# A new order for the first quarter of a hand-ordered kernel (Mamba-2 SSD followed by a SwiGLU feed-forward, one Trainium2 core)

## The chip, the cores and the metric

The kernel runs on one core of one Trainium2 chip. A core has five engines that run at the same time, each one its own instructions strictly in the order in which they stand: TensorE (PE: matrix products and transposes into PSUM), VectorE (DVE), ScalarE (ACT), GpSimd (POOL) and SyncE (SP), which here does nothing but issue DMA transfers. An instruction waits on semaphores for its inputs, and everything behind it on its engine waits with it. The metric is the device time of one launch in microseconds. Before the change it is 396.28 us, the median of three runs (396.26 to 396.57).

## What is computed

Two blocks in a row. The first is a chunked state-space scan over 4 batches, 8 heads, 768 tokens, head size 32 and state size 16; its output, with the heads side by side, is the 3072 x 256 input of a feed-forward block with an RMS norm, a gate and a value product to 1536, and a product back to 256.

```python
for c in range(nc):                                   # chunks of one sequence
    cum = np.cumsum(la, axis=-1)                      # la = log(clip(a))
    L = np.exp(cum[:, :, :, None] - cum[:, :, None, :]) * causal
    M = np.einsum('bhin,bhjn->bhij', Cc, Bc) * L
    y[:, :, sl] = M @ xc + (Cc @ state) * np.exp(cum)[..., None]
    state = decay_full * state + sum_j(Bc_j xc_j * decay_from_j)
...
xn = x / np.sqrt(np.mean(x * x, axis=-1, keepdims=True) + 1e-06) * rms_g
g, val = xn @ w_gate, xn @ w_val
out = (g / (1 + np.exp(-g)) * val) @ w_out
```

The weights come as 64-bit floats, two 32-bit words each, and the kernel makes 32-bit floats of them itself.

## The kernel before

The 3072 tokens are done in 6 blocks of 512. While a block's feed-forward products run, the scan of the next block is made. Block 0 is special: its scan and the making of the weights stand in front of everything.

**What sets the order.** The body of the kernel is a string of 1630 steps (`order`, from line 1254), each written `block:kind.numbers`, with `/slot` for the pair of PSUM banks that a step takes and `*n` for n filler products. A loop at its end (line 1417) calls the function of each step in turn, and each function emits its instructions on its engines. No scheduler changes this: on each engine the instructions stand in the order of the steps. Steps of block 0 are looked up in `first_kinds` (line 1168), the others in `kinds` (line 1231).

**Loads.** All stand on SP's queue. `bc.p` (line 125) loads B and C of a pair of 128-token chunks, `x.p` (line 132) the inputs x, `fetch.k` (line 164 or 167) one of 18 pieces of the weights: pieces 0 and 1 hold 128 columns of gate and value each, 2 to 11 hold 256 columns of gate (even) or value (odd), 12 to 17 two row groups of the output weight. SP has eight semaphores for its transfers, used in turn, so each transfer is issued only when the one eight places ahead of it has landed.

**Weights.** `man.k` (line 216 and 219, VectorE, two instructions) makes the mantissas of a piece, `pow.k` (line 197, ScalarE, three instructions) its powers of two, and `wt.k` (line 225, VectorE) their product, which is the weight. A product of the feed-forward waits for the `wt` of its piece.

**Scan of block 0.** `sums`, `exp`, `g`, `L` make the decays and the scores of a pair of chunks, `A` and `S` the states, `y.p` the outputs; `sq.p` and `yt.p` take y out of PSUM, `ms.0`, `rs.0` and `xn.0` are the norm. `scale.p` (line 514) multiplies B with its decays, `rowout.k` (line 1138) copies a row of sums and stores it to DRAM for later blocks, `turn`, `T`, `Tt`, `Td` transpose B and C.

**Feed-forward of block 0.** `early.f.s` (line 855) multiplies the not yet normed y of half s with gate and value columns of group f (0 and 1); `norm.f` applies the norm afterwards. `gate.f` (line 845, f from 2 to 5) does the normed products of four more groups; `silu.f` and `hid.f` finish them. Groups 6 to 11 go in three pairs j = 3, 4, 5 by a Strassen-like scheme of seven products of half the size, `P.k.j` (line 931): `take` (ScalarE, line 937) and `C` (VectorE, line 943) gather the partial sums, `silug` and `hidg` finish them. The scheme needs sums of weights, `cw.j.k` (line 900), and of inputs, `tx.b.k` (line 908). The letter p at the end of a kind (`cwp`, `txp`, `hidgp`) puts the same operation on GpSimd instead of VectorE. `o.f` (line 963) multiplies with the output weight.

**Into block 1.** `y.3`, `sq.3`, `yt.3`, `ms.1`, `rs.1` (which stores the roots to DRAM), `rb.1` (four loads that spread them, line 818) and `xn.1` (line 827) lead to the first products `1:P` of block 1.

Of the kernel before, what the change touches and what calls it, by code (L numbers as in the profile page):

```python
# [20 lines left out]
def kernel(  # L21
# [1202 lines left out]
    def of_chunk(n, fn):  # L1224
# [32 lines left out]
        0:mask.1.1/2 0:gcol 0:part 0:fetch.2 0:after 0:part2 0:tmask 0:sel 0:upto 0:mean 0:mid
        0:mask.0.1/1 0:mids 0:la0 0:log4.4.2 0:log4.0.4 0:r.0 0:log 0:after2 0:x.1 0:upto2 0:parts.0
        0:d 0:dx 0:eps 0:scale.0 0:middles 0:c*2 0:turn.0 0:fetch.1 0:sums.0.1 0:cx 0:Tb.0 0:exp.0.1
        0:sums.0.0 0:exp.0.0 0:turn.1 0:Tt.1.0 0:Tt.1.1 0:T.0 0:T.1 0:last.0 0:g.0.1/1 0:Tl.0  # L1260
# [6 lines left out]
        0:dT.3 0:xn.0 0:turn.2 0:norm.0 0:T.2 0:turn.3 0:T.3 0:Tt.3.1 0:fetch.4 0:dT.2 0:man.5  # L1267
        0:early.1.1 0:fetch.9 0:exp.2 0:Tt.2.0 0:fetch.7 0:wt.3 0:wt.5 0:Tt.2.1 0:norm.1 0:tx.0.0
        0:Tt.3.0 0:Td.3 0:Td.2 0:man.4 0:fetch.6 0:gate.2/0 0:silu.0 0:hid.0 0:gg.2/1 0:L1.2.3
        0:L1.2.2 0:L.2.0 0:pow.4 0:wt.4 0:man.7 0:gate.3/2 0:pow.7 0:wt.7 0:ydone.1 0:fetch.11  # L1270
        0:cwp.1.0 0:man.9 0:man.8 0:gate.4/1 0:silu.2 0:hid.2 0:x.2 0:pow.8 0:wt.8 0:txp.0.1 0:pow.9
        0:man.6 0:A.2 0:silu.3 0:x.3 0:wt.9 0:pow.6 0:hid.3 0:gate.5/0 0:S.2 0:cwp.4.0 0:silu.4
        0:scale.3 0:table.1 0:y.2/2 0:hid.4 0:silu.5 0:wt.6 0:cwp.3.0 0:hid.5 0:ydone.0 0:tx.0.2
        0:pow.11 0:S.3 0:cw.3.1 0:man.11 0:sq.2 0:bc.4 0:switch.1 0:P.2.3 0:switch.0 0:P.1.3 1:dT.0
        0:take.1.3 0:C.11.3 0:P.1.4 0:take.1.4 0:P.2.4 0:C.11.4 0:yt.2 0:x.4 0:silu.1 0:P.6.3
        0:take.6.3 0:cwp.3.2 0:tx.0.3 0:cw.4.1 0:fetch.10 0:gg.3/2 1:table 0:wt.11 0:P.5.3 0:P.7.3
        0:cwp.3.3 0:man.10 0:pow.10 0:wt.10 0:bc.5 0:cwp.5.0 0:take.7.3 0:C.22.3 0:fetch.14
        0:silug.22.3 0:silug.11.4 0:L1.3.3 0:P.5.4 0:L1.3.2 0:P.6.4 0:take.6.4 0:scale.5 0:L.3.0
        0:P.4.3 0:silug.21.3 0:P.3.3 0:scale.4 0:hidgp.11.4 0:cwp.4.2 0:fetch.12 0:pow.12
        0:hidg.21.3 0:cw.4.3 0:x.5 0:C.12.3 0:silug.12.3 0:y.3/2 0:silug.11.3 0:P.7.4 0:take.7.4  # L1280
        0:cw.5.1 1:dT.1 0:cwp.5.2 1:S.0 0:fetch.15 0:P.1.5 0:P.2.5 0:hidg.12.3 0:cwp.5.3 1:spread.0
        0:P.4.4 0:fetch.13 0:spread.10 0:take.1.5 0:P.6.5 0:table.0 0:spread.11 1:S.1 0:C.11.5
        0:C.22.4 0:sq.3 0:yt.3 0:ms.1 0:rs.1 0:cwp.1.2 0:man.12 0:take.6.5 0:P.5.5 0:wt.12 0:cwp.1.1
        0:hid.1 0:P.3.4 0:man.13 0:hidgp.11.3 1:turn.1 0:silug.21.4 0:P.7.5 0:take.7.5 1:spread.1
        0:o.0/2 0:cw.0.0 0:hidg.22.3 0:man.15 0:o.1 0:P.4.5 0:C.22.5 0:hidg.21.4 0:pow.13 0:wt.13
        0:P.3.5 0:C.12.4 0:silug.22.4 0:hidgp.22.4 0:man.14 0:silug.21.5 0:silug.22.5 0:silug.11.5
        0:C.12.5 0:pow.14 0:hidg.21.5 0:fetch.17 0:pow.15 0:o.2 0:cw.0.1 0:rb.1 0:o.3 0:xn.1 1:P.1.0
        0:silug.12.5 0:wt.14 0:hidgp.11.5 0:man.17 1:bc.0 1:take.1.0 1:P.1.1 0:tx.1.0 1:P.2.1 1:T.1
        0:txp.1.1 0:o.4 0:tx.1.2 1:take.1.1 1:P.6.1 0:pow.17 1:cw.2.0 0:hidgp.22.5 0:tx.1.3 1:C.11.1
        1:silu.11.1 1:P.6.0 1:sub.0 1:P.2.0 0:wt.15 0:wt.17 1:turn.0 1:C.11.0 0:cwp.0.2 1:Tt.1.0  # L1290
        1:hid.11.1 1:take.6.0 1:P.7.0 1:take.7.0 1:take.6.1 1:silu.11.0 1:P.5.1 1:P.5.0 1:P.4.0
        1:C.22.0 0:cwp.0.3 0:fetch.16 1:silu.21.0 0:spread.9 1:P.7.1 1:P.3.0 1:cwp.2.2 1:hid.21.0
        0:ydone.3 0:silug.12.4 1:take.7.1 1:hid.11.0 1:cwp.2.1 0:o.5 1:P.1.3 1:Tt.1.1 1:Td.1
        0:cw.1.3 1:C.22.1 1:P.4.1 1:bc.1 1:P.3.1 0:man.16 0:hidg.12.5 0:o.6 0:o.7 1:T.0 1:Tt.0.0
        0:subp.9 1:twop.2 0:hidg.12.4 0:pow.16 0:subp.11 1:take.1.3 1:C.12.0 1:silu.12.0 1:silu.21.1
        1:hidp.12.0 1:silu.22.0 1:hid.21.1 0:wt.16 1:two.0 1:two.1 1:x.0 1:silu.22.1 1:two.4
        1:C.12.1 1:twop.6 1:hid.22.0 0:ex.9 1:P.2.3 1:P.1.2 1:C.11.3 1:P.6.3 1:ex.0 1:silu.11.3
        1:P.2.2 1:take.1.2 1:P.5.3 1:hid.11.3 1:silu.12.1 1:scale2.1 1:take.6.3 1:P.7.3 1:take.7.3
        1:C.22.3 1:hid.12.1 0:o.8 1:P.6.2 0:sub.10 1:twop.3 1:take.6.2 1:C.11.2 1:two.9 1:P.4.3
        1:silu.21.3 1:two.8 1:cwp.2.3 1:hid.21.3 0:o.9 1:P.1.4 1:silu.11.2 1:hid.11.2 1:spread.3  # L1300
        1:sub.3 1:ex.3 1:P.3.3 1:take.1.4 1:twop.5 1:Tt.0.1 1:Td.0 1:C.12.3 1:silu.12.3 1:hidp.12.3
        0:ex.10 2:dT.0 1:P.5.2 1:P.6.4 1:take.6.4 1:P.7.2 1:take.7.2 0:ex.11 1:P.2.4 0:o.10 0:o.11
        1:C.22.2 1:silu.22.2 1:spread.2 1:P.4.2 1:two.10 1:silu.22.3 0:spread.8 0:subp.8 0:put.0
        1:P.3.2 0:put.1 0:put.2 1:hidp.22.1 0:ydone.2 1:C.11.4 1:silu.11.4 1:P.5.4 1:P.7.4 1:sub.2
        1:silu.21.2 1:hid.21.2 1:hid.11.4 1:hidp.22.3 0:put.3 0:ex.8 0:exps 1:hidp.22.2 1:scale2.0
        2:dT.1 1:P.1.5 1:g 1:C.12.2 1:ex.2 1:L1.3 1:take.1.5 1:P.6.5 1:take.7.4 1:C.22.4 1:twop.7
        1:silu.22.4 1:P.2.5 1:P.4.4 1:take.6.5 1:L 1:L1.2 1:P.7.5 1:y.0 1:C.11.5 1:silu.21.4
        1:hid.21.4 1:x.1 1:silu.11.5 1:P.5.5 1:two.11 1:take.7.5 1:hid.22.4 1:O.2.0 1:hid.11.5
        1:silu.12.2 1:hidp.12.2 1:u.0 1:P.4.5 1:silu.21.5 1:O.2.1 1:O.15.0 1:O.15.1 1:w.0 1:w.2
        1:C.22.5 1:silu.22.5 2:S.0 1:y.1 1:hid.21.5 1:u.1 1:O.3.0 1:u.2 2:bc.1 1:u.3 1:O.3.1 2:S.1  # L1310
        1:O.0.0 1:O.0.1 2:spread.2 2:spread.1 1:subp.1 1:P.3.5 1:C.12.5 1:sq 1:up.4 1:w.4 1:O.17.0
        1:O.17.1 1:yt 1:silu.12.5 1:hid.12.5 1:w.5 1:up.5 1:ms 1:rs 1:hidp.22.5 1:P.3.4 1:C.12.4
        1:w.10 1:O.6.0 1:O.6.1 1:O.16.0 1:O.16.1 2:turn.1 2:turn.0 1:u.9 1:silu.12.4 1:O.4.0 1:O.4.1
# [145 lines left out]
```

## Time and profile before

| what | value |
|---|---|
| median of three runs | 396.28 us |
| the profiled execution: its time / its span | 397.5 us / 395.8 us |
| PE busy | 387.3 us (98%) |
| VectorE busy | 287.4 us (73%) |
| ScalarE busy | 233.6 us (59%) |
| GpSimd busy | 155.5 us (39%) |
| granted TensorE clock | 1.00 throughout |
| chain that ended last, PE's share | 80% |

All times of day below are microseconds from the start of the span of this one execution. PE is busy 98% of the span, but its busy time is modelled from the first to the last of pipelined products, so a busy PE is not always a PE at its full rate. A `P` step, two products over 256 columns that the profile counts as four, takes 0.86 us where nothing holds it up; where the next one starts later than that, PE was held up though it counts as busy. The shares of the other engines are averages over stages that differ: VectorE is at 94 to 99% from 10 to 90 us and far lower afterwards.

### The profile page before, as it was taken

How to read it: one execution, taken by the hardware profiler on the slowest of the kernel's cores; microseconds unless marked ns; L12 is line 12 of the kernel's file. 1: busy time of each engine (PE TensorE's matmuls, PEld its weight loads, DVE VectorE, ACT ScalarE, POOL GpSimd, SP SyncE). 2: the span in 40 equal slices, each digit the busy share in tenths (PEclk: the TensorE clock that was granted, in tenths of full speed). 3: DMA queues.
4: the chain of work that ended last, by engine and by line, in shares of the span. 5: the costliest groups of instructions: out<-in, count | busy, mean ns of one | idle time of the engine just before them, and what ended most of it. 6: DMA issues, size and time to landing. Idle time of an engine off the chain costs nothing.

```text
span 395.8 us, 9624 instructions
## 1 busy us (share of the span) xinstructions
PE 387.3 (98%) x3833; PEld 333.0 (84%) x3833; DVE 287.4 (73%) x594; ACT 233.6 (59%) x483; POOL 155.5 (39%) x172
## 2 busy tenths in 40 slices
...
GB/s 101 189 165 295 181 216 190 132 154 71 23 1 68 57 87 131 84 2 30 107 36 82 13 2 68 2 15 36 42 1 3 0 8 27 55 0 2 2 2 53
DMA packets 92533, 27.01 MB, mean 68 GB/s; under 512 B 77416, under 2 KB 86344, under 8 KB 92488
## 3 DMA queue, kind: packets, MB, share of 16 engines
...
q10 hardware_dynamic: 2080, 0.13, 0.4%
...
## 4 chain that ended last, share of the span: by engine, by line
PE 80%; DVE 7%; ACT 6%; issue 2%; SPq 2%; DMA 2%; POOL 0%; DVEq 0%; ACTq 0%
PE gate L931 28%; PE o L1052 20%; PE val L931 20%; PE o L963 5%; PE y L716 3%; ACT e L197 3%; DMA wr<-in_moe_w_val_dram 2%; PE g L579 1%; SPq L125 1%; DVE wgv L225 1%; DVE m L219 1%; PE tp L529 1%; ACT u L197 1%; DVE L L618 1%; DVE ob L1083 1%
## 5 line engine op out<-in xcount | busy, mean ns | idle before, releaser
L943 DVE TENSOR_TENSOR c<-val,p 128x512 f32<-128x512 f32 x99 | 67.3, 686 | 40.4 <-PE val L931 28.6
L937 ACT COPY p<-gate 128x512 f32<-128x512 f32 x99 | 56.7, 583 | 57.1 <-PE gate L931 55.6
L956 POOL TENSOR_TENSOR hid<-c 128x256 f32<-128x256 f32 x40 | 33.6, 847 | 90.4 <-ACT c L197 88.2
L931 PE MATMUL gate<-tx,wgv 128*128 128x256 f32 x264 | 65.9, 382 | 0.0
L197 ACT ACTIVATE c<-c 128x256 f32<-128x256 f32 x99 | 39.1, 415 | 30.5 <-DVE c L943 30.1
L931 PEld LDWEIGHTS gate<-tx,wgv 128*128 128x128 f32 x264 | 48.9, 190 | 7.2 <-issue 0.3
L956 DVE TENSOR_TENSOR hid<-c 128x256 f32<-128x256 f32 x59 | 28.5, 492 | 16.9 <-ACT c L197 16.9
L1083 DVE TENSOR_TENSOR ob<-ob,o 128x128 f32<-128x128 f32 (+1 forms) x90 | 24.4, 298 | 21.1 <-PE o L1052 17.7
L482 POOL TENSOR_SCALAR_AFFINE_SELECT L<-L 64x512 f32<-64x512 f32 (+1 forms) x36 | 28.2, 783 | 21.7 <-ACT L L197 19.0
L1052 PE MATMUL o<-two,hid 128*128 128x128 f32 x280 | 36.3, 276 | 0.3 <-DVE ob L1083 0.2
L1052 PEld LDWEIGHTS o<-two,hid 128*128 128x128 f32 x280 | 34.4, 192 | 1.5 <-DVE ob L1083 0.4
L931 PE MATMUL val<-tx,sw 128*128 128x256 f32 x132 | 34.0, 382 | 0.0
L931 PE MATMUL val<-xn,sw 128*128 128x256 f32 x132 | 33.7, 380 | 0.0
L931 PE MATMUL val<-xn,wgv 128*128 128x256 f32 x132 | 33.3, 380 | 0.2 <-ACT u L197 0.2
L931 PE MATMUL gate<-tx,sw 128*128 128x256 f32 x132 | 33.4, 381 | 0.0
L931 PE MATMUL gate<-xn,wgv 128*128 128x256 f32 x132 | 32.9, 379 | 0.0
L197 ACT ACTIVATE u<-gate 128x256 f32<-128x256 f32 (+1 forms) x37 | 14.8, 403 | 22.8 <-PE gate L931 20.9
L931 PEld LDWEIGHTS val<-tx,sw 128*128 128x128 f32 x132 | 24.8, 190 | 4.0 <-DVE c L943 0.5
L931 PEld LDWEIGHTS val<-xn,wgv 128*128 128x128 f32 x132 | 24.9, 190 | 3.6 <-ACT u L197 0.3
L931 PEld LDWEIGHTS gate<-tx,sw 128*128 128x128 f32 x132 | 24.6, 190 | 3.4 <-issue 0.2
L931 PEld LDWEIGHTS gate<-xn,wgv 128*128 128x128 f32 x132 | 24.6, 190 | 3.2
L931 PEld LDWEIGHTS val<-xn,sw 128*128 128x128 f32 x132 | 24.5, 190 | 3.2 <-issue 0.2
...
## 6 DMA issues: line engine op xcount, KB each, us to landing
...
```

What stands on the lines that cost most here:

```text
L125: queue.dma_start(out=st[p][name][:, i], in_=src[b, :, sl, :].rearrange("h s n -> s h n"))
L197: nc.scalar.activation(**operands)
L219: nc.vector.scalar_tensor_tensor(out=f, in0=lo.bitcast(U32), scalar=2.0 ** -32, in1=m, op0=ALU.mult, op1=ALU.add)
L482: nc.gpsimd.affine_select(out=L[r], in_=L[r], pattern=[[0, L.shape[1]], [1, HC]], compare_op=ALU.is_ge, fill=0.0, base=0, channel_multipli ...
L716: nc.tensor.matmul(out=y[2 * k + u][rows, (2 * n + i) * HC:(2 * n + i + 1) * HC], start=(k, u, rows.start) not in opened, stop=True, skip_ ...
L931: nc.tensor.matmul(out=dst[:, half[w]], lhsT=lhsT, rhs=rhs, start=(k in (1, 2, 5) and w == 0), stop=True, skip_group_check=True)
L937: nc.scalar.copy(out=t, in_=Xs[j])
L943: nc.vector.tensor_tensor(out=t, in0=Zs[j], in1=a, op=ALU.add)
L956: engine.tensor_tensor(out=hid[:, 2 * j + c // 10 - 1, c % 10 - 1], in0=u, in1=src[:, half[1]], op=ALU.mult)
L963: nc.tensor.matmul(out=o, lhsT=hid[:, f, k // 2, (k % 2) * P:(k % 2 + 1) * P], rhs=wo[:, f], start=opens, stop=(f == NF - 1), skip_group_c ...
L1052: nc.tensor.matmul(out=Os[blk, b][:, place * P:(place + 1) * P], lhsT=hidden_or_sum(u)[:, g], rhs=rhs, start=(blk, b) not in opened, stop= ...
L1083: nc.vector.tensor_tensor(out=o, in0=o, in1=src, op=ALU.add if what[0] == "+" else ALU.subtract)
```

## The change

Only the string `order` is changed, and of it only the steps up to the 401st; the 1229 steps behind stand as before. The first 13 stand as before too. In between are the same steps in another order, 20 of them on another engine:

- from VectorE to GpSimd, 13: `tx.0.0`, `tx.0.2`, `cw.3.1`, `cw.4.1`, `cw.4.3`, `cw.5.1`, `hidg.22.3`, `hidg.12.5`, `cw.0.1`, `cw.1.3`, `tx.1.0`, `tx.1.3` and `cw.2.0`;
- from GpSimd to VectorE, 7: `cwp.3.2`, `cwp.3.3`, `cwp.5.3`, `hidgp.11.3`, `hidgp.22.5`, `cwp.1.2` and `cwp.2.2`.

SP's queue before: `bc.0 bc.1 x.0 fetch.0 gcol fetch.2 x.1 fetch.1 bc.2 fetch.5 rowout.1 fetch.3 bc.3 rowout.0 fetch.8 fetch.4 fetch.9 fetch.7 fetch.6 fetch.11 x.2 x.3 bc.4 x.4 fetch.10 bc.5 ...`. After: `bc.0 bc.1 fetch.2 x.0 fetch.0 gcol x.1 fetch.4 fetch.1 fetch.3 rowout.1 fetch.5 bc.3 bc.2 fetch.6 x.2 rowout.0 fetch.8 fetch.9 x.3 fetch.7 bc.5 fetch.10 fetch.11 x.4 bc.4 ...` (transfers of rows left out).

```diff
-        0:idle.7 0:x.0 0:hmask 1:exps 0:head 0:fetch.0 0:never 0:whole16 0:mask.0.0/0 0:aT
...
-        0:S.0 0:last.1 0:row.1 0:L.0.0 0:mask.1.0/1 0:sums.1.0 0:man.2 0:rowout.1 0:wt.0 0:exp.1.0
...
-        0:y.1/2 0:pow.2 0:sq.0 0:yt.0 0:sq.1 0:man.1 0:row.0 0:rowe.0 0:r.1 0:parts.1 0:early.0.0/0
-        0:bc.3 0:yt.1 0:ms.0 0:wt.2 0:scale.2 0:sums.3/1 0:pow.1 0:sums.2/2 0:pow.5 0:exp.3
-        0:rowout.0 0:rs.0 0:tok 0:fetch.8 0:tokout 0:man.3 0:pow.3 0:early.0.1 0:wt.1 0:early.1.0/1
...
+        0:idle.7 0:after 0:never 0:fetch.2 0:whole16 0:mean 0:part 0:head 0:part2 0:sel 0:after2
+        0:mask.0.0/0 0:upto 0:mid 0:upto2 0:eps 0:aT 0:la0 0:hmask 0:x.0 0:mask.0.1/1 0:mids
...
+        0:A.1 0:y.0/1 0:pow.0 0:S.1 0:y.1/2 0:wt.0 0:sq.0 0:yt.0 0:wt.2 0:parts.1 0:sq.1 0:row.0
+        0:rowe.0 0:pow.1 0:early.0.0/0 0:fetch.6 0:ms.0 0:dT.2 0:rs.0 0:dT.3 0:yt.1 0:man.1
+        0:sums.3/1 0:exp.3 0:pow.3 0:sums.2/2 0:early.0.1 0:x.2 0:man.3 0:wt.1 0:rowout.0 0:xn.0
+        0:norm.0 0:scale.2 0:pow.5 0:early.1.0/1 0:wt.3 0:exp.2 0:turn.3 0:man.5 0:T.3 0:Tt.3.0
...
+        0:hid.4 0:wt.8 0:txp.0.0 0:txp.0.1
+        0:pow.7 0:wt.7 0:cwp.3.0 0:cwp.3.1 0:gate.5/0 0:silu.5 0:hid.5 0:y.2/2 0:scale.5 0:cwp.4.0
+        0:cwp.4.1 0:ydone.1 0:pow.10 0:switch.1 0:P.2.3 0:switch.0 0:P.1.3 0:S.3 0:sq.2 0:fetch.11
...
```

More of the change, by code (lines that the diff above doesn't have):

```diff
@@ L1255 @@
         0:warm 0:a 0:set 0:bc.0 0:ident 0:bc.1 0:bc2.1.1 0:ones 0:zeros 0:ident16 0:whole 0:kinks
-        0:idle.7 0:x.0 0:hmask 1:exps 0:head 0:fetch.0 0:never 0:whole16 0:mask.0.0/0 0:aT
[L1257 to L1260, printed above, removed]
@@ L1267 @@
[L1267 to L1272, printed above, removed]
@@ L1273 @@
[L1273 to L1313, printed above, removed]
@@ L1415 @@
-        5:w.25 5:put.2
+        0:idle.7 0:after 0:never 0:fetch.2 0:whole16 0:mean 0:part 0:head 0:part2 0:sel 0:after2
+        0:mask.0.0/0 0:upto 0:mid 0:upto2 0:eps 0:aT 0:la0 0:hmask 0:x.0 0:mask.0.1/1 0:mids
+        0:log4.0.4 0:log4.4.2 0:mask.1.1/2 0:fetch.0 1:exps 0:tmask 0:r.0 0:parts.0 0:log 0:d 0:c*2
+        0:dx 0:turn.0 0:gcol 0:sums.0.1 0:scale.0 0:sums.1.1 0:cx 0:scale.1 0:sums.0.0 0:Tb.0 0:T.0
+        0:log4.6.2 0:x.1 0:fetch.4 0:fetch.1 0:turn.1 0:exp.0.1 0:exp.0.0 0:last.0 0:g.0.1/1
@@ new lines @@
+        0:fetch.3 0:Tl.0 0:man.2 0:Tt.1.0 0:cc 0:Tt.1.1 0:middles 0:g.0.0/0 0:T.1 0:exp.1.1 0:A.0
+        0:last.1 0:L.0.1 0:S.0 0:L.0.0 0:row.1 0:rowout.1 0:mask.1.0/1 0:sums.1.0 0:man.0 0:g.1.1/0
+        0:Tl.1 0:pow.2 0:rowe.1 0:exp.1.0 0:fetch.5 0:bc.3 0:L.1.1 0:g.1.0/2 0:bc.2 0:L.1.0 0:r.1
+        0:A.1 0:y.0/1 0:pow.0 0:S.1 0:y.1/2 0:wt.0 0:sq.0 0:yt.0 0:wt.2 0:parts.1 0:sq.1 0:row.0
+        0:rowe.0 0:pow.1 0:early.0.0/0 0:fetch.6 0:ms.0 0:dT.2 0:rs.0 0:dT.3 0:yt.1 0:man.1
+        0:sums.3/1 0:exp.3 0:pow.3 0:sums.2/2 0:early.0.1 0:x.2 0:man.3 0:wt.1 0:rowout.0 0:xn.0
@@ new lines @@
+        0:norm.0 0:scale.2 0:pow.5 0:early.1.0/1 0:wt.3 0:exp.2 0:turn.3 0:man.5 0:T.3 0:Tt.3.0
+        0:early.1.1 0:norm.1 0:wt.5 0:Tt.3.1 0:Td.3 0:turn.2 0:T.2 0:Tt.2.1 0:Tt.2.0 0:Td.2 0:man.4
+        0:gate.2/0 0:gg.2/1 0:silu.0 0:hid.0 0:L.2.0 0:fetch.8 0:gate.3/2 0:ydone.0 0:L1.2.2
+        0:fetch.9 0:x.3 0:pow.4 0:fetch.7 0:silu.2 0:L1.2.3 0:wt.4 0:A.2 0:pow.6 0:hid.2 0:gate.4/1
+        0:bc.5 0:man.8 0:S.2 0:silu.3 0:fetch.10 0:hid.3 0:pow.9 0:man.6 0:wt.6 0:scale.3 0:pow.8
+        0:cwp.1.0 0:tok 0:tokout 0:man.9 0:wt.9 0:man.7 0:silu.4 0:hid.4 0:wt.8 0:txp.0.0 0:txp.0.1
@@ new lines @@
+        0:man.13 0:wt.13 0:ydone.3 0:o.1 1:dT.1 0:cwp.1.1 0:P.3.4 0:hidg.21.4 1:turn.1 1:T.1
+        1:Tt.1.1 1:cwp.2.0 0:hidgp.22.3 1:sub.0 1:turn.0 0:P.3.5 1:cwp.2.1 0:silug.11.5 0:o.2
+        1:cw.2.2 0:o.3 0:hidgp.22.4 0:man.14 0:silug.21.5 0:rb.1 0:xn.1 0:C.12.5 1:P.1.1 0:pow.14
+        0:hidg.21.5 0:pow.15 0:fetch.16 0:hidgp.11.5 1:P.2.1 0:silug.12.5 0:C.12.4 0:txp.1.0
+        0:txp.1.1 1:take.1.1 1:C.11.1 1:table 1:P.1.0 1:P.2.0 0:hidgp.12.5 0:spread.11 0:cw.1.2
+        1:P.5.1 0:tx.1.2 1:take.1.0 1:C.11.0 0:wt.15 0:cwp.0.1 1:Tt.1.0 1:P.6.0 1:silu.11.1 1:P.6.1
```

238 lines of the change are left out of this document (135 added, 103 removed).

## The prediction

> **What bounds the kernel now.** I began with the busy times of the engines in stretches of 10 us (columns: stretch, length, then busy us and instructions of PE, PE's weight loads, VectorE, ScalarE, GpSimd, then clock, share of the DMA engines, GB/s).
>
> ```profile
> core 0: us, PE busy (x) PEld busy (x) DVE busy (x) ACT busy (x) POOL busy (x), PEclk, DMA share, GB/s
> ...
> 20.00:30.00 10.00, 8.60 (x139) 6.17 (x132) 9.38 (x21) 8.90 (x15) 3.95 (x4) 1.00 0.83 165
> ...
> 50.00:60.00 10.00, 9.59 (x191) 7.73 (x191) 9.63 (x24) 8.32 (x19) 3.50 (x4) 1.00 0.95 218
> ...
> 80.00:90.00 10.00, 10.00 (x50) 8.81 (x49) 9.73 (x16) 8.06 (x15) 5.56 (x6) 1.00 0.93 159
> 90.00:100.00 10.00, 10.00 (x48) 8.81 (x47) 6.74 (x15) 7.72 (x18) 4.63 (x5) 1.00 0.22 76
> ```
>
> PE is at its limit from the sixties on. Until 90 us VectorE is nearly full too, then it has room. So the end of the kernel is the moment at which PE becomes steadily busy plus the products left; the change touches only what lies ahead. I then read PE's timeline for the places where that moment is set (start, length, then the idle time before and what ended it).
>
> ```profile
> 29.91 1.97 PE L855 MATMUL gate<-yt,wgv 128*128 128x256 f32 x8 [0.84 <-DVE wgv L225]
> ...
> 50.25 0.89 PE L716 MATMUL y<-T,S 32*64 32x64 f32 x32
> ...
> 52.40 1.10 PE L931 MATMUL val<-xn,wgv 128*128 128x256 f32 x4 [0.16 <-ACT u L197]
> ...
> 57.21 0.70 PE L579 MATMUL g<-T 32*64 32x128 f32 x32 [0.26 <-ACT yt L787]
> ...
> 63.53 0.46 PE L716 MATMUL y<-T,S 32*64 32x64 f32 x24 [0.24 <-DVE L L618]
> ```
>
> `early.1.0` starts at 29.91, the first `P` at 52.40, and from `y.3` at 63.53 no wait of PE follows that matters. The rest is VectorE's timeline: what held `early.1.0`, and the one later place where PE is fed just in time, `xn.1`.
>
> ```profile
> 26.08 0.42 DVE L514 TENSOR_TENSOR Bd<-br,d_sb 128x256 f32<-128x256 f32 x1
> 26.42 0.28 DVE L1138 COPY r_sb<-r_ps 128x128 f32<-128x128 f32 x1
> 27.07 0.43 DVE L216 TENSOR_SCALAR m<-wr 128x512 int32<-128x512 int32 x1 [0.37 <-DMA wr<-in_moe_w_val_dram]
> 27.54 0.69 DVE L219 SCALAR_TENSOR_TENSOR m<-wr,m 128x512 f32<-128x512 uint32 x1
> 28.14 1.62 DVE L225 SCALAR_TENSOR_TENSOR wgv<-m,e 128x512 f32<-128x512 f32 x1
> ...
> 80.75 1.41 DVE L827 SCALAR_TENSOR_TENSOR xn<-yt,gcol,sq 128x512 f32<-128x512 f32 x2 [0.20 <-DMA sq<-roots]
> ```
>
> The `wt.1` for which PE waits stands behind `man.3`, which waited for piece 3 (issued at 23.05). It takes 1.62 us where the same form elsewhere takes 0.68, beside GpSimd's masks of L (27.95 to 30.78).
>
> **The change, part by part.** Steps of an engine are counted from start to start, as its timeline has them: `man` 1.06 us, `wt` 0.60, half an `L` 1.13, `parts` 1.70, a pair of `yt` 0.8, `pow` 2.2, a 256-column add on VectorE 0.33.
>
> *Loads.* Through `x.1` the same transfers stand on SP, piece 2 now ahead of x.0. A piece of 512 KB moves in some 1.4 us (at the 385 to 397 GB/s of the stretch from 36 to 40 us), so x.0, moved by 9.5 before, is there by about 11; the PE product that needs it, `A.0`, ran at 13.14 and comes at about 13.5. That hides the delay with 2 us to spare; were it gone, each us would be lost in full. Pieces 4 and 3 and later x.2, x.3 come earlier, B and C of pairs 3 and 2 later: bc.2 by 28 to 29 against its use at 32.6 (`turn.2`). Piece 11 now waits on SP for `pow.8` (about 45), with x.4, bc.4 and piece 12 behind it: some 9 us of transfers bring x.5 to about 57, and `y.3` needs it at 63. I cost the loads at nothing, and keep +1.4 (x.0 late by one piece in full) for the range.
>
> *VectorE up to `wt.1`.* Piece 3 lands at about 20 instead of 27, which ends the wait of 0.37; `scale.2` (0.34) and the copy of `rowout.0` (0.28) are moved behind `wt.1`: from 26.08 to 27.07, 0.99 us, goes. Walked from `parts.0` (ends 8.7 in both): four products of `scale` 1.3, `Tb` and `T` 0.94, `man.2` 1.07, the row sum 0.5, a wait for `g.0.1` until 12.65 (PE now does a third `sums` first, 0.45), then `L`, states, `L`, copy, `man.0`: 17.1; `L`, `L`, states 20.2; `wt.0` (its `pow.0` now ends at about 20.35), `yt`, `wt.2`, `parts.1`, `yt`: 24.85; `man.1`, `man.3`: `wt.1` starts at 26.97, 1.17 earlier. `exp.3`, behind which GpSimd makes those masks, also comes about 1 us earlier, so I leave `wt.1` its 1.6 us. `rs.0` no longer stands behind `pow.5` and `exp.3` (3.1 us) and ends near 26, ahead of its use. So `early.1.0` starts at 28.75 instead of 29.91.
>
> *PE from there to the first `P`.* 22.49 us before; the same work, and the 0.43 of `tok`, which now stands in this stretch. VectorE's share of it, from the end of `wt.1` to `C.11.3`, was 26.9 us (29.7 to 56.6); it loses `man.11` 1.06 and `tx.0.0`, `tx.0.2`, `cw.3.1` 1.0, and gains `scale.5`, `scale.2` and the copy, 1.0: 25.8, so it keeps ahead of PE and some of PE's shortfall goes (1.5 us: 21.0 of work in 22.49). I take half a us of it to pay for `tok`: first `P` at 51.3, **1.1 us earlier**.
>
> *The first `P` steps.* 52.40 to 65.29 is 12.9 us for 11 `P` steps (9.5), `gg.3` (0.65) and `y.3` (1.83): 0.9 us short. `gg.3` now stands one `P` later and `y.3` two, behind what they waited for. **0.8 us** of it goes; between 0 and 0.9.
>
> *From VectorE to GpSimd.* Net six operations: 6 x 0.33 = 2.0 us off a VectorE that is full until 90 us, and 6 x 0.73 to 1.23 us (rows of those forms) on GpSimd, which is 35 to 56% busy there. What this is worth in itself is nothing: it lets VectorE keep up with a PE that is 2 us earlier. The cover is GpSimd's room. Four sums of weights in a row (`cwp.3.0` to `cwp.4.1`) now begin only with `wt.7` at about 50.7 and end at 53.8 (at 1.2 us each 55.5); `P.6.4` wants the last at 55.6.
>
> The trace has both outcomes of an overlap of the two engines: `wt.1` at 1.62 for 0.68, and `man.1` at its normal 0.69 (22.39) while GpSimd's add beside it took 1.15 instead of 0.81. The Trainium skill (SBUF — State Buffer, section Who interferes with whom) says that a VectorE instruction with two inputs in SBUF and a GpSimd one that reads SBUF exclude each other for a whole instruction, whichever starts first; it speaks against this part, and the rows agree that one of the two loses, though not by a whole instruction. By that rule, estimated at half of 0.73 lost for each of six more overlaps, 2.2 us would be shared between the two engines, and the gain below would shrink to about 1.
>
> *Into block 1.* `xn.1` waited for the spread roots (80.75) and PE wanted it at 82.05. Now PE comes at 82.05 - 1.9 + 0.44 (`turn.0` of block 1 is moved ahead) = 80.6. On SP, two loads of L and piece 17 stood between the store of the roots and their spread; now it is piece 14 and one small load, so the roots are there by about 78, and VectorE reaches `xn.1` at 78.5 to 79. It holds, by 1.5 us.
>
> **Sum.** 1.1 + 0.8 = 1.9 us off the profiled execution's 397.5 (span 395.8 and 1.7 around it): 395.6. That execution stands 1.2 above the median of 396.28, so against the median: **394.4 us**. Its own range: nothing of the second term and half of the first, 395.7; all of PE's shortfall between 29.91 and 65.29 (2.45) and the earlier start (1.2), 392.6.
>
> **Rivals.** (a) *The head start is lost at the next joint.* `o.2` waits for `wt.13`, and that for `pow.13` behind two table loads (1.28 each): by my count 76.4 against PE's 77.1, thin. If this or `xn.1` comes as in before, PE waits there and at most 0.7 us stay: 395.9. For it: VectorE at 97% from 70 to 90; against: its load falls. (b) *Slower: GpSimd and VectorE in each other's way.* Place: 50 to 80 us, where GpSimd gets the added sums while VectorE is full. Price: the held-up rows lost 0.42 (`m` 1.10 for 0.69) to 0.94 (1.62 for 0.68); at 0.6, six added operations cost VectorE 3.6, less the 2.0 taken off it: +1.6, and as `xn.1` is then VectorE's, the head start is gone: 397.9. It decides once `xn.1` ends later than 82.05. Against it: over 52 to 82, with 20 GpSimd operations, VectorE lost only 2.2 us in all by such stretching. (c) *x.0 late.* The 1.4 us of the piece go through to `A.0` and the states: 1.1 + 0.8 - 1.4 = 0.5 gained, 395.8. (d) *The change doesn't do what it says*: the order is the program's on every engine, so this has no chance.
>
> **How the numbers follow.** Forecast 0.54, (a) 0.14, (b) 0.25, (c) 0.07. The time is the forecast's, 394.4. The range reaches from 392.6 (all shortfall gone) to 397.9, the price of (b); the forecast's own is 392.6 to 395.7. What a measurement of this kernel can tell from no change is about 0.2%, 0.8 us. Faster: the forecast, most of it, and the better edge of (a) and (c), 0.61. Same: the rest of these, 0.13. Slower: (b) and what I have overlooked, 0.26.
>
> **What would show it.** Right: `early.1.0` near 28.7, the first `P` near 51.3, no PE wait ahead of `gg.3` and `y.3`, the first product of block 1 near 80.5, and everything behind it some 2 us earlier. Wrong: VectorE waiting for A or x ahead of 14 us, many stretched VectorE rows between 50 and 80, a PE wait at `P.6.3`, `P.6.4`, `o.2` or the first product of block 1.

## The result, and the profile after

| what | before | after |
|---|---|---|
| median of 22 runs each, on the same chip | 396.7 us (395.85 to 398.15) | 395.23 us (394.39 to 397.59) |
| ratio after to before | | 0.9968, 95% interval 0.9956 to 0.998 |
| the profiled execution: its time / its span | 397.5 / 395.8 us | 397.3 / 395.6 us |

The change makes the kernel faster by 1.3 us (0.8 to 1.75). The times of the changed kernel fall into two groups: 17 of the 22 between 394.39 and 395.39, five between 396.22 and 397.59. The granted clock does not tell the groups apart: it is 0.999 or 1.000 in all but one of the 22, which ran at 0.996 (397.59 us). The profiled execution is one of the five. It shows where such an execution loses, and the experiments show the others.

VectorE, PE and ScalarE first, by the stretches of 10 us used before (same columns).

```profile
core 0: us, PE busy (x) PEld busy (x) DVE busy (x) ACT busy (x) POOL busy (x), PEclk, DMA share, GB/s
20.00:30.00 10.00, 9.95 (x137) 7.51 (x126) 9.83 (x19) 8.61 (x13) 5.15 (x4) 1.00 0.88 157
30.00:40.00 10.00, 8.35 (x54) 4.34 (x54) 8.97 (x15) 8.34 (x15) 4.01 (x5) 1.00 0.98 246
```

Between 20 and 30 us PE gained (8.60 busy before), between 30 and 40 both PE and VectorE have gaps that they didn't have (before: 10.00 and 9.93). PE's timeline of the same execution shows where:

```profile
25.10 4.01 PE L855 MATMUL gate<-yt,wgv 128*128 128x256 f32 x16
...
31.57 3.60 PE L845 MATMUL gate<-xn,wgv 128*128 128x512 f32 x8
36.42 0.45 PE L579 MATMUL g<-T 32*64 32x128 f32 x8 [1.25 <-DVE hid L866]
37.27 0.98 PE L579 MATMUL g<-T 32*64 32x128 f32 x24 [0.39 <-DVE T L553]
...
51.08 1.16 PE L931 MATMUL val<-xn,wgv 128*128 128x256 f32 x4
...
56.65 0.69 PE L579 MATMUL g<-T 32*64 32x128 f32 x32
...
63.59 0.59 PE L716 MATMUL y<-T,S 32*64 32x64 f32 x24
...
69.83 0.41 PE L800 MATMUL ms<-sq,mean 128*32 128x128 f32 x4 [0.23 <-POOL sq L768]
...
81.94 1.13 PE L931 MATMUL gate<-xn,wgv 128*128 128x256 f32 x4
83.29 0.89 PE L931 MATMUL val<-xn,wgv 128*128 128x256 f32 x3 [0.23 <-DVE c L943]
```

`early.1.0` is the second half of the first row: it follows `early.0.1` without a gap, at 27.15 instead of 29.91. Then two new waits, 1.64 us in all, stand at `gg.2`. The first `P` comes at 51.08 (before 52.40). `gg.3` (56.65) and `y.3` (63.59) no longer wait, and two more `P` steps are done ahead of `y.3`. At `ms.1` and at the first products of block 1 there are new gaps. VectorE's timeline of the same stretch and of `xn.1`:

```profile
26.32 0.68 DVE L225 SCALAR_TENSOR_TENSOR wgv<-m,e 128x512 f32<-128x512 f32 x1
...
31.24 0.43 DVE L514 TENSOR_TENSOR Bd<-br,d_sb 128x256 f32<-128x256 f32 x1 [0.96 <-DMA br<-in_B_dram]
31.58 0.69 DVE L225 SCALAR_TENSOR_TENSOR wgv<-m,e 128x512 f32<-128x512 f32 x1
32.18 1.37 DVE L216 TENSOR_SCALAR m<-wr 128x512 int32<-128x512 int32 x1
33.58 1.50 DVE L219 SCALAR_TENSOR_TENSOR m<-wr,m 128x512 f32<-128x512 uint32 x1
35.01 0.68 DVE L866 TENSOR_TENSOR u<-gate,sq 128x512 f32<-128x512 f32 x1
...
81.13 1.42 DVE L827 SCALAR_TENSOR_TENSOR xn<-yt,gcol,sq 128x512 f32<-128x512 f32 x2 [0.45 <-DMA sq<-roots]
```

`scale.2` waits 0.96 us for B of pair 2, and `man.5` behind it (32.18 and 33.58) takes 2.87 us where the same two instructions take 1.11 in the run ms_later below, beside GpSimd's masks (31.70 to 34.54). `norm.1` (35.01) is what PE waits for.

**The lead.** To follow the gain through the kernel I counted, for each moment, the products that PE has still to do (0.2155 us each, transposes 0.11), and took the difference to the profiled execution of before; this difference is called the lead. It counts feed-forward products and transposes alone, so a scan step that has moved shows for a while: at 52 us the kernel before is still at `y.2`, until 52.40, which makes every lead there some 0.4 us too small, and at 66 us rest_only and no_swaps have yet to do `y.3`, so their leads there are too large. From 100 us on the two orders are the same and the lead stays as it is: 397.5 less the lead gives each execution's time within 0.4 us.

| execution (its time) | 52 us | 66 | 74 | 84 | 100 |
|---|---|---|---|---|---|
| changed kernel (397.3) | 0.9 | 1.7 | 0.6 | -0.2 | 0.0 |
| again (396.52) | 1.1 | 1.9 | 0.9 | 0.7 | 0.9 |
| scale2_late (394.92) | 2.6 | 3.5 | 2.4 | 2.4 | 2.4 |
| ms_later (395.26) | 2.4 | 3.2 | 2.2 | 2.0 | 2.2 |
| both_moves (394.83) | 2.6 | 3.5 | 2.6 | 2.4 | 2.4 |
| both_look1 (394.78) | 2.8 | 3.7 | 2.6 | 2.6 | 2.6 |
| both_look2 (396.22) | 1.3 | 2.2 | 1.1 | 0.9 | 1.1 |
| bc_first_both (396.05) | 1.5 | 2.4 | 1.5 | 1.3 | 1.3 |
| dt_first (396.42) | 1.1 | 1.9 | 0.9 | 0.9 | 0.9 |
| front_only (396.61) | 2.2 | 0.9 | 0.7 | 0.9 | 0.9 |
| rest_only (398.36) | 0.2 | 1.1 | -0.9 | -0.9 | -1.1 |
| late_to_vector (398.08) | 2.6 | 3.5 | 2.4 | 0.9 | -0.9 |
| no_swaps (402.94) | 0.9 | 0.0 | -2.6 | -2.6 | -5.8 |

### The profile page after: what moved, and what is told of

Read it like the earlier page. It is cut to its first block, busy times and chain, and to the rows that moved or that the text cites. A ratio compares the mean times of both kernels' runs of the same rounds, so it can differ in the third digit from the quotient of the medians.

```text
span 395.6 us, 9626 instructions
## 1 busy us (share of the span) xinstructions
PE 387.5 (98%) x3833; PEld 331.9 (84%) x3833; DVE 287.7 (73%) x588; ACT 233.6 (59%) x483; POOL 160.8 (41%) x178
## 4 chain that ended last, share of the span: by engine, by line
PE 77%; DVE 10%; ACT 3%; issue 3%; DMA 3%; SPq 3%; DVEq 0%; ACTq 0%
PE gate L931 26%; PE o L1052 21%; PE val L931 19%; PE o L963 3%; PE y L716 2%; SPq L125 2%; DVE m L219 2%; DMA sq<-roots 1%; DMA br<-in_B_dram 1%; PE g L579 1%; DVE m L216 1%; ACT L L197 1%; DVE wgv L225 1%; DVE S L668 1%; DVE c L943 1%
## 5 line engine op out<-in xcount | busy, mean ns | idle before, releaser
L956 DVE TENSOR_TENSOR hid<-c 128x256 f32<-128x256 f32 x59 | 30.1, 519 | 17.8 <-ACT c L197 17.8
L482 POOL TENSOR_SCALAR_AFFINE_SELECT L<-L 64x512 f32<-64x512 f32 (+1 forms) x36 | 29.3, 813 | 19.9 <-ACT L L197 13.1
```

What stands on the lines that cost most here:

```text
L482: nc.gpsimd.affine_select(out=L[r], in_=L[r], pattern=[[0, L.shape[1]], [1, HC]], compare_op=ALU.is_ge, fill=0.0, base=0, channel_multipli ...
L956: engine.tensor_tensor(out=hid[:, 2 * j + c // 10 - 1, c % 10 - 1], in0=u, in1=src[:, half[1]], op=ALU.mult)
```

## The experiments

All are the changed kernel with some steps of the string elsewhere, or under the other engine's name. Median, spread and number of runs are given; the kernel before ran on the same chip each time, and ratios are to it.

**again.** No edit.

> The changed kernel once more, unaltered. In its first profile PE's remaining work (products left, 0.2155 us each) was 1.7 us ahead of the kernel before at 64 to 66 us, and nothing was left of that at 84: 0.65 went at ms.1 (69.2 to 70.2), 0.3 before P.4.5 (73.0), 0.7 at the first products of block 1 (81.9 to 83.3). That execution took 397.3 us, the median of its runs is 395.23. Theory 1: the loss at 82 to 84 is that of one execution, in which the spread roots landed late (80.93); a profile of an ordinary execution shows them landing by 80.0, and a lead of 1 us or more from 84 on. Theory 2: the loss is in every execution and the 2 us between profile and median are the profiling itself; then this profile shows the same gaps again. Time: 395.2 us, ratio 0.997.

Measured: 396.22 us (394.58 to 397.58, 12 runs), before 397.33, ratio 0.9963 (0.994 to 0.9986). Again two groups: six times up to 395.92, six from 396.52. The profile, from the lower edge of the upper group, has the same wait at `scale.2` (0.79 instead of 0.96) and at `gg.2`; `xn.1` does not wait for the roots (80.28), and a lead of 0.9 us stays. So the loss at 82 to 84 us (0.7) is that of one execution, as theory 1 has it, but the lead that it put at 1 us or more was 0.9 here, since the wait at 31 us was there too.

**scale2_late.**

```diff
-0:norm.0 0:scale.2 0:pow.5
+0:norm.0 0:pow.5
...
-0:norm.1 0:wt.5 0:Tt.3.1
+0:norm.1 0:wt.5 0:scale.2 0:Tt.3.1
```

> The changed kernel with one step moved: scale.2 (VectorE, 0.43 us, waited 0.96 us for the load of B of pair 2 at 31.24) goes behind wt.5. Theory 1: wt.3, man.5 and norm.1 start 0.9 to 1.4 us earlier, PE's waits at gg.2 (1.25 and 0.39) go, gate.3 starts at 36.8 to 37.3 instead of 38.18 and the first P at 50.0 to 50.6 instead of 51.08; at the end 394.2 to 394.8 if the joints into block 1 pass it on. Rival: those joints (ms.1, xn.1 behind the roots) are set by ScalarE's row of work and the roots' round trip, not by PE; then the first P is earlier, the lead is gone by 84 us, and the time is 395.2. Second rival: VectorE is full up to 90 us, so what is late next is A.2 or the copies T.2; then the first P stays at 51.1.

Measured: 396.91 us (394.92 to 397.86, 12 runs), ratio 0.9975 (0.9955 to 0.9996). In the profile (394.92) the wait and both gaps of PE are gone, the first `P` is at 49.24, and a lead of 2.4 us reaches the end. But eight of 12 times are 396.4 and above: as a kernel it is not better than the changed one. What makes the two groups is not this step's place alone.

**no_swaps.**

```diff
-0:cwp.3.0 0:cwp.3.1 0:gate.5/0 0:silu.5 0:hid.5
+0:cwp.3.0 0:cw.3.1 0:gate.5/0 0:silu.5 0:hid.5
...
-0:yt.2 0:cw.3.2 0:x.4
+0:yt.2 0:cwp.3.2 0:x.4
...
```

> The changed order with every one of its 20 operations back on the engine that it had in the kernel before (13 back to VectorE, 7 back to GpSimd); the order of the steps stays. Theory 1 (the prediction's): the exchange lets VectorE keep up; without it VectorE has six more operations of 0.33 us before 90 us, 2.0 us in all, and xn.1 or a product before it comes 0.5 to 2 us later: 395.7 to 397.2. Rival (b) of the prediction: GpSimd's added sums hold up VectorE by more than they relieve it; then this is faster than the changed kernel, 394.0 to 394.8. Rival: neither, 395.2.

Measured: 402.96 us (402.74 to 405.65, 6 runs), ratio 1.0149 (1.0117 to 1.0181): 6.7 us above the changed kernel in the same comparison. First VectorE, then PE in its profile:

```profile
51.19 0.93 DVE L900 TENSOR_TENSOR sw<-sw,wgv 128x256 f32<-128x256 f32 x1 [1.30 <-POOL sw L900]
```
```profile
52.77 3.00 PE L931 MATMUL gate<-xn,wgv 128*128 128x256 f32 x8 [2.13 <-DVE hid L878]
...
61.06 1.10 PE L931 MATMUL gate<-tx,wgv 128*128 128x256 f32 x4 [1.39 <-ACT e L197]
```

`cw.3.1` adds to what `cwp.3.0`, right ahead of it, makes on GpSimd. On GpSimd it simply follows; on VectorE it waits 1.30 us for the other engine, with `hid.5` and all else queued behind it, and PE waits 2.13. Behind that wait the granted clock falls to half for some 3 us (columns as in the table of stretches above):

```profile
54.00:57.00 3.00, 3.00 (x9) 2.34 (x8) 1.75 (x4) 2.01 (x7) 2.58 (x4) 0.50 0.76 256
```

An estimate from that row is that some 1.6 us of the 6.7 are this lower clock; the mean clock is 0.996 in all six runs, and 0.004 of the 401.2 us of the span is as much. Why it fell is not shown: behind PE's waits of 1.80 us in front_only and 1.72 in rest_only it stayed at 1.00. So this run does not price VectorE's load (VectorE was waiting at several places), it prices, with the clock, operations taken from the engine for which their place was chosen. Hence late_to_vector below.

**front_only** (the new order up to the first `P`, before's order behind it) **and rest_only** (the reverse).

> The order of the changed kernel up to the first P, then the steps that are left in the order (and on the engines) of the kernel before. Theory 1: the first P comes at 51.1 (before 52.40), and the P section passes 1.1 to 1.3 us of that on to y.3; ms.1 and the roots come from before's order, in which the roots' spread landed 0.2 us after VectorE was ready; roots 1 us earlier, and 395.3 to 395.7 us at the end. Rival (a): the head start is lost at xn.1, since the roots' round trip is not PE's: 396.5 to 396.9, as before. Rival: before's P section waits for sums that the new front leaves later (scale.5 and cw.4.1 are already done, man.11, tx.0.2 and S.3 not), slower than before.

> The mirror of the run that had only the new front: the order of the kernel before up to its first P, then the steps that are left in the changed kernel's order and on its engines. In front_only the first P came 3 us earlier than in before and all but 0.4 to 0.9 us of it was gone by 56 us, since PE waited 1.8 us for a product of the third P (P.1.4) whose PSUM was not yet taken out. Theory: the new front and the new P section are worth something only together; here the P section starts at 52.4 and passes its 0.8 us (the prediction's term) on, so the lead on before is 0.5 to 1.0 us at 66 us and 0 to 0.7 at 84 (ms.1 costs 0.65 in the changed order): 396.3 to 397.3 on a chip where before has 397.3. Rival: the section needs the front's earlier sums (pow.10, cw.4.1, scale.5 are late here) and loses: 398 or more. Rival: the section is where the whole gain comes from; lead 1.5 us or more at 84.

Measured: front_only 396.52 us (396.08 to 399.46, 12 runs), ratio 0.9994 (0.9971 to 1.0018); rest_only 398.56 (397.91 to 400.69, 12 runs), ratio 1.0031 (1.0012 to 1.005). The step that waits in front_only is the fifth `P` (`P.6.3`), not `P.1.4` as the expectation of rest_only says. PE and then ScalarE of front_only:

```profile
55.28 0.89 PE L931 MATMUL gate<-tx,sw 128*128 128x256 f32 x3 [1.80 <-ACT p L937]
```
```profile
50.40 1.48 ACT L197 ACTIVATE e<-e,kinks 128x512 f32<-128x512 int16 x2
51.79 0.76 ACT L197 ACTIVATE e<-wr,kinks 128x512 int16<-128x512 int16 x1
52.58 1.48 ACT L197 ACTIVATE e<-e,kinks 128x512 f32<-128x512 int16 x2
...
54.54 1.08 ACT L937 COPY p<-gate 128x512 f32<-128x512 f32 x2
```

At the seam `pow.10` (already in the new front) and `pow.11` (in the old rest) both stand ahead of `take.1.3`, 2.2 us more on ScalarE, and PE waits for the `take`. rest_only has the same two ahead of its `take.1.3` (`pow.11` in the old front, `pow.10` in the new rest), and PE waits 1.72 us there at 57.27. By the starts of PE's rows, front_only is 2.97 us ahead of before at the first `P` (49.43) and 0.76 once `y.3` is done; rest_only goes from 0.55 ahead to 0.78 late in the same stretch. Neither part brings by itself what they bring together, but both halves are charged for one seam: these runs do not give the price of a part.

**late_to_vector.**

```diff
-0:cwp.4.3 1:cwp.2.0 0:hidgp.22.3 0:txp.1.0 0:hidgp.12.5 0:cwp.0.1 0:cwp.1.3 0:txp.1.3
+0:cw.4.3 1:cw.2.0 0:hidg.22.3 0:tx.1.0 0:hidg.12.5 0:cw.0.1 0:cw.1.3 0:tx.1.3
```

> The changed kernel with eight of its 13 moved operations back on VectorE, those behind 65 us, which stand in no chain with a neighbour on GpSimd (cw.4.3, cw.2.0 of block 1, hidg.22.3, tx.1.0, hidg.12.5, cw.0.1, cw.1.3, tx.1.3); the seven that came to VectorE stay. This puts 8 x 0.33 = 2.6 us more on VectorE between 68 and 92 us. Theory (the prediction's): VectorE is full there and reaches xn.1 later by the share ahead of it (cw.4.3, cw.2.0, hidg.22.3: 1.0 us), and the products behind by up to 2.6: 1 to 2.5 us slower than the changed kernel. Rival (b): GpSimd's operations cost VectorE 0.42 to 0.94 each in stretched rows, as much as they take off it; then it is no slower, or faster by up to 1 us.

Measured: 398.6 us (398.08 to 401.38, 12 runs), ratio 1.0052 (1.0031 to 1.0073). Its profile is of the fastest of the twelve runs; five are from 400.07 up, and no profile shows what these lose. Up to 74 us its lead is like that of scale2_late, which has the same front in time, and it loses 3.3 us by 100. PE in its profile:

```profile
81.00 1.13 PE L931 MATMUL gate<-xn,wgv 128*128 128x256 f32 x4 [0.99 <-DVE xn L827]
...
87.50 1.96 PE L931 MATMUL gate<-tx,sw 128*128 128x256 f32 x8 [1.46 <-DVE sw L900]
```

These two waits of PE are for VectorE. For these eight, rival (b) is out: on GpSimd they are worth 3.3 us of lead, a little more than their 2.6 us on VectorE. The other 12 exchanged operations were not tried by themselves.

**ms_later and both_moves.**

```diff
-0:ms.1 0:silug.21.4 0:rs.1 0:take.7.5 0:P.5.5
+0:take.7.5 0:silug.21.4 0:P.5.5 0:ms.1 0:rs.1
```

> The changed kernel with ms.1 (8 small products on PE) and rs.1 put one P step later, behind P.5.5, and take.7.5 ahead of them. In three profiles of the changed order PE lost 0.6 to 0.7 us at ms.1, whose second half waited for GpSimd's sum of squares. Theory: that wait goes, since the sum is done by then; the table load ahead of rs.1 on ScalarE covers the later ms.1, the roots are stored at most 0.5 us later, and VectorE still reaches xn.1 no earlier than the roots: lead on the changed kernel 0.6 us at 74 and at 100 us, median 0.5 lower. Rival: xn.1 waits for the roots (they were 0.45 late in the first profile), so the lead is gone at 84 and the time is that of the changed kernel.

> Both small moves: scale.2 behind wt.5 and ms.1, rs.1 behind P.5.5. Theory: the lead on the profiled execution of before (397.5 us) is 3.4 us at 66 us as in scale2_late, and stays at 3.0 or more from 74 on, where scale2_late kept 2.4; lowest times 394.2 to 394.4 against 394.6 of the changed kernel, median at least 0.5 below it. Rival: what one move gives the next joint takes (xn.1 behind VectorE's row of work, which the earlier PE doesn't shorten): lead 2.4 at 84, times as scale2_late.

Measured: 396.11 us (394.88 to 397.53, 12 runs), ratio 0.9974 (0.9955 to 0.9993), and 396.87 (394.81 to 397.58, 12 runs), ratio 0.9974 (0.9954 to 0.9994). The move did not pay. PE in ms_later:

```profile
68.22 1.13 PE L931 MATMUL val<-tx,sw 128*128 128x256 f32 x4 [0.64 <-DVE c L943]
```

`P.5.5` now waits 0.64 us for `C` on VectorE, as much as was lost at `ms.1`: VectorE's row of work was late there in either order. Neither theory had named this. `xn.1` ran at 78.99 with no wait for the roots, so the first rival does not hold either.

ms_later is the changed kernel unaltered up to 66 us, and its profile is of the lower group. There `scale.2` did not wait:

```profile
30.47 0.41 DVE L514 TENSOR_TENSOR Bd<-br,d_sb 128x256 f32<-128x256 f32 x1
30.80 0.68 DVE L225 SCALAR_TENSOR_TENSOR wgv<-m,e 128x512 f32<-128x512 f32 x1
31.40 0.42 DVE L216 TENSOR_SCALAR m<-wr 128x512 int32<-128x512 int32 x1
31.86 0.69 DVE L219 SCALAR_TENSOR_TENSOR m<-wr,m 128x512 f32<-128x512 uint32 x1
32.47 0.68 DVE L866 TENSOR_TENSOR u<-gate,sq 128x512 f32<-128x512 f32 x1
```

`norm.1` starts at 32.47 instead of 35.01, and the first `P` at 49.49 instead of 51.08, though `scale.2` itself came only 0.77 earlier. SP's queue shows why it did. First the profiled execution of the changed kernel, then ms_later, then both_look2 (below); the row is the second half of `bc.3`, with the time for which its issue stood in the queue:

```profile
21.25 3.38 SPq L125 DMA_DIRECT2D br<-in_B_dram  x1
```
```profile
20.78 2.15 SPq L125 DMA_DIRECT2D br<-in_B_dram  x1
```
```profile
21.38 3.99 SPq L125 DMA_DIRECT2D br<-in_B_dram  x1
```

The row ends at 24.6, 22.9 and 25.4 us. By the eight semaphores used in turn, the issue would wait there for the gate half of piece 1, eight transfers ahead; the profiles have no landing of that transfer, so this cause is argued and not shown. What they show is that the row's end goes with the first `P`: in the five profiles with the changed front and its engines it ends at 22.9 to 24.0 where the first `P` is at 49.2 to 49.5 (ms_later, front_only, late_to_vector), and at 24.3 and 24.6 where it is at 50.8 and 51.1 (again and the first one). All of `bc.2`, the store of the decays, piece 6 and `dT` stand behind it.

**both_look1, both_look2.** The kernel of both_moves twice more.

> The kernel of both_moves once more, for a profile of another execution. If its time is 396.4 or more, the trace shows where an execution of the upper group loses its 2.3 us; theory 1: ahead of the first P (first P 1 us or more later than the 49.2 of the lower group), by a load that is late between 25 and 50 us. Theory 2: behind 84 us, or at the roots' spread.

> The same kernel a third time, with the same two theories: an execution of the upper group has its first P at 50.2 or later (theory 1), or at 49.2 and loses behind it (theory 2); one of the lower group repeats the lead of 2.4 us at 84.

Measured: 394.78 and 396.22 us. The first repeats both_moves. The second is late, and VectorE shows by what:

```profile
36.26 0.76 DVE L553 TENSOR_TENSOR T<-tp,dT 128x256 f32<-128x256 f32 x2 [0.96 <-DMA dT<-rowe]
```

With `scale.2` out of the way, it is the next load in the late queue, `dT`. PE waits 0.94 at `gg.2` and the first lead of 2.8 us is 1.3. Theory 1 holds for this execution: the loss lies ahead of the first `P`, behind a late load.

**bc_first_both.** Kernel of both_moves, with

```diff
-0:fetch.5 0:bc.3 0:L.1.1 0:g.1.0/2 0:bc.2
+0:bc.3 0:L.1.1 0:g.1.0/2 0:bc.2 0:fetch.5
```

> The kernel of both_moves with the load of piece 5 put behind those of pairs 3 and 2 of B and C on SP. The times of the changed kernel and of its three variants fall into two groups about 2.3 us apart (394.4 to 395.7, and 396.4 to 397.9); the two profiles from the upper part had B of pair 2 late by 0.8 to 1.0 us at scale.2, and those from the lower group had it in time. Theory 1: how late the loads between 17 and 28 us come decides the group, and piece 5, 512 KB ahead of the pairs, is what delays them; here the pairs land 1.3 us earlier (a piece of 512 KB at 385 to 397 GB/s), man.5 finds piece 5 just in time at 30.8, and nearly all times fall into the lower group: median 395 or less. Theory 2: the group is decided elsewhere (both_moves has it too, though scale.2 no longer stands ahead of anything), and the split stays: median 396 to 397. Rival: piece 5 is late at man.5 by up to 1 us, and the lower group moves up by as much.

Measured: 395.51 us (394.85 to 396.05, 7 runs), before 396.46, ratio 0.9971 (0.9958 to 0.9984). No time of the upper group, as theory 1 said, but the lower group is moved up a little, as the rival said. Its profile (the slowest of the seven), ScalarE and VectorE:

```profile
30.23 0.78 ACT L197 ACTIVATE e<-wr,kinks 128x512 int16<-128x512 int16 x1 [2.05 <-DMA wr<-in_moe_w_val_dram]
```
```profile
34.68 0.42 DVE L553 TENSOR_TENSOR T<-tp,dT 128x256 f32<-128x256 f32 x1 [0.98 <-DMA dT<-rowe]
```

Piece 5 is now what ScalarE waits for (`pow.5`), and `dT` is late still. The kernel that was edited, both_moves, had seven upper times of 12, so seven runs without one say something. But the execution at 396.05 has a lead of 1.3 us at the end, close to the 1.1 of both_look2 at 396.22, so it is not shown that late executions are gone.

**dt_first.** Kernel of both_moves, with

```diff
-0:fetch.6 0:ms.0 0:dT.2 0:rs.0 0:dT.3
+0:ms.0 0:dT.2 0:rs.0 0:dT.3 0:fetch.6
```

> The kernel of both_moves with the load of piece 6 (512 KB) put behind the two loads dT of decays instead of ahead of them; piece 5 stays ahead of the pairs. In the profile of both_moves at 396.22 us the SP queue stood 3.99 us ahead of a half of bc.3 (2.20 at 394.83), everything behind it came 1.6 to 2.6 us later, and VectorE waited 0.96 us for dT at 36.26; with piece 5 behind the pairs the times were 394.85 to 396.05, and ScalarE waited 2.05 us for piece 5 and VectorE 0.98 for dT. Theory: dT behind a piece of 512 KB is what such an execution waits for; without the piece it lands 1 to 2 us earlier, VectorE's wait goes, and the times gather at 394.3 to 395.5, median 395.0 where before has 396.5, none above 396.4. Rival: the queue is late as a whole (it waits for the landing of piece 1, four places ahead), so the next load in it is waited for instead (x.2, the pieces 8 and 4), and the two groups stay as they were in both_moves.

Measured: 396.66 us (394.79 to 397.96, 12 runs), before 396.97, ratio 0.9977 (0.9955 to 0.9999). Both groups are back, five times up to 395.26 and seven from 396.42. VectorE's wait for `dT` is gone, and the rival's sentence came true (VectorE, then ScalarE):

```profile
41.25 0.43 DVE L216 TENSOR_SCALAR m<-wr 128x512 int32<-128x512 int32 x1 [1.12 <-DMA wr<-in_moe_w_gate_dram]
```
```profile
43.02 0.77 ACT L197 ACTIVATE e<-wr,kinks 128x512 int16<-128x512 int16 x1 [1.79 <-DMA wr<-in_moe_w_val_dram]
```

The queue is late as a whole; taking one load out of its way hands the wait to the next piece. No variant beats the changed kernel by more than the scatter: the ratios to before are 0.9968 and 0.9963 for it, and 0.9971 to 0.9977 for the five variants that keep its engines and both its parts. A version that always has its loads in time was not found, and what makes the queue late in some executions stays open.

## Why the prediction was right, and where its terms were not

The forecast was 394.4 us and the measured median 395.23. Of the 0.8 between them, 0.4 is the reference: the forecast took 1.9 off a median of three runs, 396.28, and over 22 runs that median is 396.7. The rest is a gain of 1.3 to 1.5 in place of 1.9. That it came so close is in part luck: the forecast had too little ahead of the first `P` and too much behind it, as the terms below show.

*What bounds the kernel* held: from 100 us on every lead stands in the time, one for one.

*VectorE up to `wt.1`.* Forecast 1.17 earlier, with `wt.1` stretched to 1.62 us as before. Measured 1.82 earlier (26.32), unstretched: 0.68. So `early.1.0` came 2.76 us earlier, not 1.16. What "I leave `wt.1` its 1.6 us" missed is which instruction comes first. GpSimd's masks, before and then after:

```profile
27.95 2.83 POOL L482 TENSOR_SCALAR_AFFINE_SELECT L<-L 64x1024 f32<-64x1024 f32 x2 [4.28 <-ACT L L197]
```
```profile
26.46 3.62 POOL L482 TENSOR_SCALAR_AFFINE_SELECT L<-L 64x1024 f32<-64x1024 f32 x2 [4.03 <-DVE m L219]
31.70 2.84 POOL L482 TENSOR_SCALAR_AFFINE_SELECT L<-L 64x1024 f32<-64x1024 f32 x2 [1.62 <-ACT L L197]
```

Before, the mask (27.95) started ahead of `wt.1` (28.14), and `wt.1` paid 0.94. After, `wt.1` (26.32) started ahead of the mask (26.46), and the mask paid: the first of the two instructions of that row took 1.55 us, 0.41 more than the 1.14 of the same one in both_look1 at 32.80. (The second took 2.01 beside `xn.0`, 27.12.) With B late, `man.5` (32.18) came behind the second pair (31.70) and paid 1.76. The Trainium skill (SBUF — State Buffer, section Who interferes with whom) says that issue order decides which of the two engines blocks; these rows agree.

*Loads at nothing.* This term failed. The text put `bc.2` at 28 to 29 against a use at 32.6. The use had become `scale.2` at 30.3, ahead of `wt.3`, `man.5` and `norm.1`, and in the profiled execution B landed at 31.14, 4.58 us after its issue at 26.56. Price: `scale.2` 0.77 later than in ms_later, and nearly 1.8 more by pushing `man.5` onto the masks, 2.54 in all at `norm.1`. Some 0.95 comes back, since `wt.5` is then clear of the masks (0.67 against 1.63 in ms_later), and 1.59 us is left at the first `P` (51.08 against 49.49). The text followed pair 2 to its use on PE and not to the step that was moved in front of it.

*PE to the first `P`.* 1.1 us forecast; 1.3 measured in the late execution (51.08), and 2.9 to 3.4 where the queue was in time (49.49, 49.24, 49.01). The first figure is two errors that cancel, so that it is near the forecast is luck.

*The first `P` steps.* 0.8 us forecast, 0.24 measured. The first product behind `y.3`, before and then after:

```profile
65.29 1.13 PE L931 MATMUL gate<-tx,wgv 128*128 128x256 f32 x4
```
```profile
65.46 1.13 PE L931 MATMUL gate<-tx,sw 128*128 128x256 f32 x4
```

Before, PE needs 12.89 us from the first `P` (52.40) to there for 11 `P` steps; after, it needs 14.38 (from 51.08) for 13. Two more steps at 0.86 would have made it 14.62. In eight of the ten executions with the new order there and its engines it is 14.37 to 14.40, and 15.14 in bc_first_both and dt_first, where PE waits 0.50 and 0.51 us for a weight. `gg.3` and `y.3` wait no more, as forecast, but their two waits were only 0.26 and 0.24 us: the text counted the whole shortfall of 0.9 as theirs. (The lead grows by 0.8 to 0.9 from 52 to 66 us, but some 0.4 of this is `y.2`, which the kernel before still has to do at 52, and the count goes in steps of 0.2.)

*From VectorE to GpSimd.* "Worth nothing in itself, it lets VectorE keep up": shown by late_to_vector, with 3.3 us of lead for eight of the operations. The price without cover was too low, and the exchange is no separate part: the places in the string presuppose it (no_swaps, 6.7 us with the lower clock).

VectorE's rows did get longer: over 52 to 82 us they were longer than the shortest of their form by 4.8 us in all in the profiled execution and 4.0 in both_look1, against 2.2 before; GpSimd's by 2.6 in all three. The Trainium skill's rule had led the prediction to an estimate of 2.2 us lost, shared by both engines. VectorE alone lost 1.8 to 2.6 more than before, so the text's argument that the rows lose little was too easy, and one of its signs of being wrong, many stretched rows, did come. But it is not shown that the exchange is what lengthens them: in late_to_vector, with 13 GpSimd operations in this stretch in place of 20, VectorE's rows are longer by 4.4. (The kernel before has 15 there, not the 20 of the text.) The exchange pays all the same, as late_to_vector shows.

*Into block 1.* The roots by 78, VectorE at 78.5 to 79, the first product near 80.5: in ms_later, scale2_late and both_moves `xn.1` starts at 78.99, 78.74 and 78.65 and waits for nothing, and the first product of block 1 comes at 80.12, 79.90 and 79.77 (before 81.93, where the text has 82.05). In the profiled execution the spread landed at 80.93, VectorE waited 0.45 and PE lost some 0.7 us; this is rival (a), in that execution. `ms.1` was in none of the text's lists, and some 0.9 to 1.1 us of lead go between 66 and 74 in every execution of the new order.

Rival (b) is refuted by late_to_vector for the eight operations that it put back, (c) by `early.0.0`, which came 1.3 us earlier than before (21.33 against 22.60). (For (a), "at most 0.7 us stay" would be 395.6 by the text's own reference, not 395.9.) The sum: in an execution whose loads are in time 2.2 to 2.6 us are gained on the profiled before; in a late one 0 to 1.1. By the starts of PE's rows the lead in both_look1 is 3.4 us at the first `P` and 3.6 once `y.3` is done, and 2.6 stay to the end; in the profiled execution these are 1.3, 1.6 and 0.0. The forecast had 1.1, 1.9 and 1.9. The median lies in the group whose loads are in time, with a larger gain ahead of the first `P` than forecast and a loss of about 1 us after `y.3` that was not forecast.
